# One placing stage for all four query blocks of a visit, value loads on SyncE's queue: a change to a fused attention and MLP kernel

## Chip, cores, metric

One core of one Trainium2 chip. The metric is the device time of the core in microseconds; each kernel was run several times beside the kernel before on the same chip.

## The reference

Attention with a threshold (8 batches, 8 heads, 576 positions, head size 64), then an MLP over 4608 tokens, all in fp32:

```python
scores = 0.125 * q @ k.T
scores = where(scores >= max(scores) - tau, scores, -1e9)
attn = softmax(scores)                    # then / (sum + 1e-9)
x = (attn @ v) laid out as (tokens, 512)
out = relu(x @ w_in) ** 2 @ w_out         # 512 -> 2048 -> 512
```

## The kernel before, in parts

Work goes in *visits*: two heads of one batch, in five steps (four blocks of 128 queries and a rest of 64). A step makes scores on TensorE, the softmax on VectorE, ScalarE and GpSimd, and fills the free time of TensorE with MLP matmuls from a list that is fixed when the program is built. The weights have to be turned (queries to columns) before the value products. From the twelfth visit on (25 visits) VectorE turns 32x32 tiles and DMAs **place** them in `wT`:

```python
def load_v(n):
    queue = nc.gpsimd if by_dma(n) else nc.sync
    ...                                     # 6 DMAs
def turn_blocks(vis, i):                    # pairs of blocks (0,1), (2,3), then the rest;
    ...                                     # two buffers in `turned`, used in turn
def place_blocks(vis, pair):
    for qb in range(4):
        for j in range(4):
            to = wT[j * 32:j * 32 + 32, :, :]
            if pair < NBLK // 2:            # 32 partitions x 9 runs of 64 floats
                nc.sync.dma_start(out=to[:, :, at:at + 64], in_=wb[rows, j::4, :, :]...)
            else:                           # the rest: 32 x (4 or 5) runs of 32 floats
                nc.sync.dma_start(out=to[:, c:c + n, at:at + 32], in_=wb[rows, first::4, 0, :])
...                                         # in step s, after the softmax of the step:
m, x = steps[s - 1]
turn_blocks(m, x)
if x >= 2:
    place_blocks(m, x - 2)                  # 16 DMAs at x = 2, 3 and 4
...                                         # end of the last step of a visit:
load_v(n + 1)
```

The value products of a visit (`mix`) stand four steps behind its last block; they read all of `wT`, so the next visit's DMAs can't start before they are done. `some_sums` makes 16 sums of MLP weights on VectorE once, just after the first of these visits.

Of the kernel before, what the change touches and what calls it, by code (L numbers as in the profile page):

```python
# [9 lines left out]
FP32 = mybir.dt.float32  # L10
# [9 lines left out]
def kernel(  # L20
# [10 lines left out]
    nc = tc.nc  # L31
    B, H, S, D = q.shape
    d_model, d_ff = moe_w_in.shape
    n_tokens = out.shape[0]
    P = 128
    HP = H // 2
    NPAIR = B * HP
    NBLK = S // P
    REST = S - NBLK * P
# [11 lines left out]
    const = ctx.enter_context(tc.tile_pool(name="const", bufs=1))  # L51
# [17 lines left out]
    WP = 512  # L69
# [3 lines left out]
    wT = const.tile([P, NC9, S], FP32, name="wT")  # L73
# [4 lines left out]
    at = RAW * 2 * WP  # L78
# [8 lines left out]
    RING = 6 * TCH  # L87
    xT = const.tile([P, NMC, RING], FP32, name="xT")
    KB = S // 32
    NB = 2 * KB * 2 * 32  # L90
    turned = const.tile([P, 2 * NB], FP32, name="turned")
    assert 3 * 3 * WP <= 2 * NB
    g = const.tile([P, NFT, TCH], FP32, name="g")
    gsum = [const.tile([P, HF, P], FP32, name=f"gsum{i}") for i in range(2)]
    p1s = const.tile([P, HD], FP32, name="p1s")
# [52 lines left out]
    def rows_of(n):  # L148
        return rows_in[n % 2 if n <= 2 * HP else 0]
# [16 lines left out]
    def load_v(n):  # L166
        b, h = divmod(visits[n][0], HP)
        h *= 2
        t = vs[n % 2]
        queue = nc.gpsimd if by_dma(n) else nc.sync  # L170
        for u in range(2):
            at = u * (NBLK + 1)
            queue.dma_start(out=t[:, at:at + NBLK, :],
                              in_=v[b, h + u, 0:NBLK * P, :].rearrange("(c p) d -> p c d", p=P))
            for half in range(2):
                queue.dma_start(out=t[half * D:(half + 1) * D, at + NBLK, :], in_=v[b, h + u, NBLK * P:S, :])

    def prep(n):

# [71 lines left out]
    def next_bank():  # L251

        among = (4, 5, 6, 7) if state["step"] > first_dma + 2 else (6, 7)
        used["bank"] = min([x for x in among if x > used["bank"]] or among)
        return bank[used["bank"]]
# [22 lines left out]
                nc.tensor.matmul(ps[rows, 0, 0:D], w[rows, 0, keys], ident[rows, rows], start=True, stop=True)  # L278
            nc.scalar.copy(wT[:, NBLK, NBLK * P:S], ps[:, 0, 0:D])

    blocks = {}
    N1 = 2 * P + REST

    def turn_blocks(vis, i):


        w = weights[vis, i][0]
        two = i < NBLK
        if not two or i % 2 == 0:
            at = len(blocks) % 2 * NB  # L290
            if two:
                wb = turned[:, at:at + NB].rearrange("p (k u q) -> p k u q", u=2, q=32)
            else:
                wb = turned[:, at:at + KB * 32].rearrange("p (k u q) -> p k u q", u=1, q=32)
            blocks[vis, i // 2] = wb
        wb = blocks[vis, i // 2]
        if two and i >= 2:

            parts = [(0, 0, KB - 2, 0), (0, KB - 2, KB, KB), (1, 0, 2, KB - 2), (1, 2, KB, KB + 2)]
        else:  # L300
            parts = [(u, 0, KB, u * KB) for u in range(2 if two else 1)]
        for u, k0, k1, at in parts:
            nc.vector.transpose(wb[:, at:at + k1 - k0, i % 2, :],  # L303
                                w[:, u, k0 * 32:k1 * 32].rearrange("p (k q) -> p k q", q=32))

    def place_blocks(vis, pair):


        wb = blocks[vis, pair]
        for qb in range(4):  # L310
            rows = slice(qb * 32, qb * 32 + 32)
            for j in range(4):
                to = wT[j * 32:j * 32 + 32, :, :]
                if pair < NBLK // 2:
                    at = pair * N1 + qb * 64
                    nc.sync.dma_start(out=to[:, :, at:at + 64], in_=wb[rows, j::4, :, :].rearrange("p c u q -> p c (u q)"))  # L316
                else:

                    first = j if qb < 2 else (j - KB) % 4
                    c = first // 4 if qb < 2 else (first + KB) // 4  # L320
                    n = len(range(first, KB, 4))
                    at = 2 * P + qb % 2 * 32
                    nc.sync.dma_start(out=to[:, c:c + n, at:at + 32], in_=wb[rows, first::4, 0, :])  # L323

    read_to = {"x": 0}

# [29 lines left out]
    def mix(n, cols):  # L356

        def term(ps, u, c, at, rows=slice(0, P), first=False, last=False):
            nc.tensor.matmul(ps[u * D:(u + 1) * D, :], vs[n % 2][rows, u * (NBLK + 1) + c, :],  # L359
                             wT[rows, NBLK if c == NBLK else u * (NBLK + 1) + c, at:at + ps.shape[1]],  # L360
                             start=first, stop=last)

        above, below = slice(0, D), slice(D, P)
        if not by_dma(n):
            ps = take("tx", (4, 5))[:, 0:cols.stop - cols.start]
            for c in range(NBLK):
                for u in range(2):
                    term(ps, u, c, cols.start, first=(c == 0))
            for u, rows in enumerate((above, below)):
                term(ps, u, NBLK, cols.start, rows, last=True)  # L370
            put(n, cols.start, ps, False)
            return
        one, two = (next_bank() for x in range(2))
        for c in range(NBLK):
            for ps, at in ((one[:, 0:N1], 0), (two[:, 0:S - N1], N1)):
                for u in range(2):
                    term(ps, u, c, at, first=(c == 0))

        for ps, at, places in ((one[:, 0:N1], 0, (above, below)), (two[:, 0:S - N1], N1, (below, above))):
            for u, rows in enumerate(places):  # L380
                term(ps, u, NBLK, at, rows, last=True)
        put(n, 0, one[:, 0:2 * P], True)
        put(n, NBLK * P, one[:, 2 * P:N1], False)
        put(n, 2 * P, two[:, 0:S - N1], True)

# [9 lines left out]
    def mlp_in(j, x):  # L395

        f, at = FORDER[x], j * TCH % RING
        if x % 2 == 0:
            used["h"] = take("mm", (6, 7)) if j < PLAIN else next_bank()
        h = used["h"].rearrange("p (f n) -> p f n", f=2)  # L400
        for c in range(NMC):
            nc.tensor.matmul(h[:, x % 2, :], w_in_sb[:, c, f * P:(f + 1) * P], xT[:, c, at:at + TCH],  # L402
                             start=(c == 0), stop=(c == NMC - 1))
        if x == NFT - 1:
            read_to["x"] = (j + 1) * TCH
        posts = []
        if j == PLAIN and state["step"] > first_dma + 1:
            posts.append(lambda: some_sums(2))
        if x % 2:
            def square():  # L410
                to = g[:, f - 1:f + 1, :]
                nc.scalar.activation(out=to, in_=h, func=AF.Relu)  # L412
                nc.gpsimd.tensor_tensor(out=to, in0=to, in1=to, op=ALU.mult)  # L413
                if j >= PLAIN and x % 8 == 7:
                    square_half(x // 8 * (HF // 2))
            posts.append(square)
        return posts
# [4 lines left out]
    def some_sums(count):  # L422

        for to, a, b, part in sums[:count]:
            f = slice(part * 2, part * 2 + 2)
            nc.vector.tensor_tensor(out=wo[:, to, f, :], in0=wo[:, a, f, :], in1=wo[:, b, f, :], op=ALU.subtract)  # L426
        del sums[:count]
# [27 lines left out]
    def product(j, x, half):  # L455
# [3 lines left out]
        to = used["p"][:, 0:HD]  # L459
        p = PRODUCTS[x]  # L460
        if sums:
            assert state["step"] > first_dma + 1
            some_sums(16 if x > 1 else 8)
        g0, g1 = g[:, 0:HF, :], g[:, HF:, :]
        left, slot = {"1": (g0[:, :, 0:P], Q00), "5": (gsum[0], FT1), "6": (gsum[1], FT2), "2": (g1[:, :, 0:P], Q10),
                      "7": (gsum[0], FT3), "4": (g1[:, :, P:], FT4), "3": (gsum[1], Q11)}[p]
# [42 lines left out]
    def by_dma(n):  # L509

        return n >= 3 * HP - 1
# [26 lines left out]
    PIECE_US = 1.76  # L538
    VALUES_US = 4.8
    waiting = deque()  # L540
    state = {"us": 0.0, "left": 0.0, "step": 0, "rounded": 0, "usable": 0, "then": [], "last": []}

    def early():
        return state["step"] < min(chunk_at)
# [77 lines left out]
    for s in range(END + 1):  # L622
# [5 lines left out]
        if on:  # L628
            n, i = steps[s]
            at = visits[n][1].index(i)  # L630
            last = at == len(visits[n][1]) - 1
            now = list(range(done, done + pieces[s]))
            done += pieces[s]
            more = n + 1 < len(visits)
            short = n < 2 * HP
            if short and at == 0 and 0 < n + 1 < 2 * HP:
                load_qk(n + 2)
            elif not short and at == 1 and more:
                load_qk(n + 1)
            if now:  # L640
                round_weights(now[0], 0)
            scores(s)
# [21 lines left out]
                add_chunk(j)  # L664
        if old:
            turn(*old, 2)
        if on:
            threshold(n, i)
            if last and more and not lay:
                prep(n + 1)  # L670
            if lay and now:
                round_weights(now[0], 1)
            if now:
                round_weights(now[0], 2)
                round_weights(now[0], 3)
            if not at_once:
                divide(n, i)
        if 0 < s <= NST and by_dma(steps[s - 1][0]):
            m, x = steps[s - 1]
            turn_blocks(m, x)  # L680
            if x >= 2:
                place_blocks(m, x - 2)
        fill(quarter)
        if on and at_once:
            divide(n, i)
# [48 lines left out]
```

## Time and profile before

| | before |
|---|---|
| time, median (range) | 1434.72 us (1434.34 to 1438.54), 3 runs |
| TensorE, VectorE, GpSimd busy | 96%, 61%, 53% |
| mean granted clock of TensorE | 0.991 |
| value products, wait for placing DMAs | 8.4 us, 5 times |

TensorE is the bound, so only its stops count. How the rows are read is told with the lines in the prediction. The list of DMA issues adds sizes and times to landing (columns: KB of one, median us from issue to landing):

```profile
wT<-turned SPq DMA_DIRECT2D x800, 72.0 KB, 2.2
...
vs<-in_v_dram POOLq DMA_DIRECT2D x50, 128.0 KB, 3.5
```

### The profile page before, as it was taken

Reading aid. Unit: us, or ns where it says so; the run is one execution under the profiler, and the core shown is the slowest. Engines: PE = TensorE matmul, PEld = TensorE weight load, DVE = VectorE, ACT = ScalarE, POOL = GpSimd, SP = SyncE. Lnnn points to the kernel's source line nnn. Section 1 sums busy time; section 2 is a strip of 40 time slices with the busy share of each in tenths; the row PEclk is TensorE's granted clock in tenths of the full one; section 3 lists DMA queues with packets and bytes.
Section 4 is the critical chain, followed back from the end, with each engine's and each line's share of the span. In section 5 each row is a group of like instructions: output and inputs, shape, how many; then the busy total and the mean of one; then the engine's idle time right before and its main releaser. Section 6 shows DMA issues by size and latency. Waiting matters only on the chain.

```text
span 1433.2 us, 22476 instructions
## 1 busy us (share of the span) xinstructions
PE 1374.8 (96%) x7460; PEld 1063.1 (74%) x7460; DVE 872.0 (61%) x1847; ACT 440.3 (31%) x1080; POOL 760.7 (53%) x1015
## 2 busy tenths in 40 slices
PE   5898999899999999999999999999999999999998
PEld 3676656677777777777777787777777877878887
DVE  5998886975766666666666666666666566401011
ACT  3765655223222323223232222222222232210100
POOL 2687887545555555655454646464546454422332
PEclk9998999999999999999999999999999999999999
DMA  7664541245555555554545555545454555310000
GB/s 149 131 141 108 130 115 41 48 79 106 90 108 94 108 98 113 99 105 87 94 87 106 92 102 98 111 86 101 81 102 89 104 95 111 67 29 12 4 15 15
DMA packets 507202, 127.14 MB, mean 89 GB/s; under 512 B 497488, under 2 KB 499088, under 8 KB 507088
## 3 DMA queue, kind: packets, MB, share of 16 engines
q1 hardware_dynamic: 496208, 107.78, 40.7%
q0 software_dynamic: 8496, 17.64, 4.0%
q8 instruction: 60, 0.98, 0.3%
q10 hardware_dynamic: 2384, 0.30, 0.1%
q14 instruction: 54, 0.44, 0.1%
HBM read 49.81 MB, written 9.44 MB: 41 GB/s over the span
## 4 chain that ended last, share of the span: by engine, by line
PE 80%; DVE 7%; SPq 5%; issue 2%; ACT 2%; DMA 1%; POOL 1%; ACTq 0%; POOLq 0%; DVEq 0%
PE bank L402 30%; PE bank L468 26%; PE s L202 12%; PE bank L359 10%; SPq L323 3%; SPq L316 2%; DVE w L230 1%; PE bank L266 1%; PE bank L436 1%; DVE st L207 1%; DVE wo L426 1%; DVE turned L138 1%; DVE turned L137 1%; ACT w L218 1%; DMA wT<-turned 1%
## 5 line engine op out<-in xcount | busy, mean ns | idle before, releaser
L402 PE MATMUL bank<-xT,w_in_sb 128*128 128x256 f32 x2304 | 521.8, 383 | 1.8 <-ACT osb L443 1.8
L402 PEld LDWEIGHTS bank<-xT,w_in_sb 128*128 128x128 f32 x2304 | 433.5, 191 | 82.8 <-issue 21.5
L207 DVE TENSOR_REDUCE st<-s 128x1 f32<-128x576 f32 x288 | 207.1, 753 | 221.1 <-PE s L202 219.7
L230 DVE SCALAR_TENSOR_TENSOR w<-s,st,w 128x576 f32<-128x576 f32 x269 | 210.1, 815 | 122.2 <-ACT w L218 122.0
L468 PE MATMUL bank<-wo,gsum 128*128 128x256 f32 x1088 | 248.7, 382 | 1.8 <-POOL gsum L392 1.7
L242 POOL TENSOR_SCALAR w<-w,st 128x576 f32<-128x576 f32 x269 | 225.8, 847 | 28.0 <-DVE st L233 21.1
L468 PEld LDWEIGHTS bank<-wo,gsum 128*128 128x128 f32 x1088 | 204.4, 190 | 40.0 <-issue 6.6
L413 POOL TENSOR_TENSOR g<-g 128x512 f32<-128x512 f32 x144 | 150.8, 1054 | 128.5 <-ACT g L412 128.2
L215 ACT ACTIVATE st<-st 128x2 f32<-128x2 f32 (+1 forms) x160 | 32.7, 204 | 603.5 <-DVE st L207 602.9
L202 PE MATMUL s<-kT,qT 64*128 64x288 f32 x1024 | 178.6, 445 | 36.0 <-DVE w L230 14.5
L468 PE MATMUL bank<-wo,g 128*128 128x256 f32 x816 | 187.9, 381 | 0.0
L359 PE MATMUL bank<-wT,vs 128*64 128x128 f32 (+7 forms) x1700 | 174.5, 358 | 11.8 <-DMA wT<-turned 8.4
L303 DVE STREAM_TRANSPOSE turned<-w 128x576 f32<-128x576 f32 (+2 forms) x325 | 167.7, 563 | 28.9 <-DMA wT<-turned 24.8
L218 ACT ACTIVATE w<-s,st 128x576 f32<-128x576 f32 x269 | 184.3, 731 | 0.6 <-issue 0.3
L468 PEld LDWEIGHTS bank<-wo,g 128*128 128x128 f32 x816 | 153.5, 190 | 28.1 <-issue 6.0
L240 POOL TENSOR_SCALAR st<-st 128x2 f32<-128x2 f32 (+1 forms) x160 | 36.8, 230 | 257.9 <-DVE w L230 247.0
L202 PEld LDWEIGHTS s<-kT,qT 64*128 64x128 f32 x1024 | 100.6, 193 | 96.0 <-issue 67.8
L359 PEld LDWEIGHTS bank<-wT,vs 128*64 128x64 f32 (+1 forms) x1700 | 101.6, 138 | 86.0 <-issue 39.0
L412 ACT ACTIVATE g<-bank 128x512 f32<-128x512 f32 x144 | 86.0, 599 | 180.1 <-PE bank L402 179.7
L482 DVE TENSOR_TENSOR gsum<-g 128x512 f32<-128x512 f32 x34 | 23.2, 715 | 109.3 <-PE bank L468 109.3
L185 POOL COPY qmid<-qT 64x64 f32<-64x64 f32 x64 | 18.7, 292 | 90.4 <-DVE qT L181 88.5
L143 POOL TENSOR_TENSOR turned<-turned 128x512 f32<-128x512 f32 x32 | 41.1, 1283 | 43.4 <-DVE turned L141 37.8
(68 smaller groups left out, 993.2 us busy)
## 6 DMA issues: line engine op xcount, KB each, us to landing
wT<-turned SPq DMA_DIRECT2D x800, 72.0 KB, 2.2
ql<-in_q_dram SPq DMA_DIRECT2D x126, 72.0 KB, 2.6
out_dram<-osb POOLq DMA_DIRECT2D x34, 256.0 KB, 2.8
wo<-in_moe_w_in_dram SPq DMA_DIRECT2D x16, 512.0 KB, 4.6
wo<-in_moe_w_out_dram SPq DMA_DIRECT2D x16, 512.0 KB, 3.8
vs<-in_v_dram POOLq DMA_DIRECT2D x50, 128.0 KB, 3.5
kl<-in_k_dram SPq DMA_DIRECT2D x63, 72.0 KB, 2.4
kl<-in_k_dram SPq DMA_DIRECT2D x63, 64.0 KB, 2.4
```

Source lines behind the costliest of these rows:

```text
L202: nc.tensor.matmul(sc[u][:, half, 0:HALF], lhsT, kT[rows, half * HALF:(half + 1) * HALF], start=True, stop=True)
L207: nc.vector.tensor_reduce(out=mx[:, u:u + 1], in_=sc[u][:, :, 0:HALF], axis=AX.XY, op=ALU.max)
L218: nc.scalar.activation(out=w[:, u, :].rearrange("p (h k) -> p h k", h=2), in_=sc[u][:, :, 0:HALF], func=AF.Exp, bias=bias[:, u:u + 1], sca ...
L230: nc.vector.scalar_tensor_tensor(out=wu, in0=sc[u][:, :, 0:HALF], scalar=thr[:, u:u + 1], in1=wu, op0=ALU.is_ge, op1=ALU.mult, accum_out=s ...
L242: nc.gpsimd.tensor_scalar(out=w[:, u, :], in0=w[:, u, :], scalar1=z[:, u:u + 1], scalar2=rcp[:, u:u + 1], op0=ALU.add, op1=ALU.mult)
L303: nc.vector.transpose(wb[:, at:at + k1 - k0, i % 2, :], w[:, u, k0 * 32:k1 * 32].rearrange("p (k q) -> p k q", q=32))
L323: nc.sync.dma_start(out=to[:, c:c + n, at:at + 32], in_=wb[rows, first::4, 0, :])
L359: nc.tensor.matmul(ps[u * D:(u + 1) * D, :], vs[n % 2][rows, u * (NBLK + 1) + c, :], wT[rows, NBLK if c == NBLK else u * (NBLK + 1) + c, a ...
L402: nc.tensor.matmul(h[:, x % 2, :], w_in_sb[:, c, f * P:(f + 1) * P], xT[:, c, at:at + TCH], start=(c == 0), stop=(c == NMC - 1))
L412: nc.scalar.activation(out=to, in_=h, func=AF.Relu)
L413: nc.gpsimd.tensor_tensor(out=to, in0=to, in1=to, op=ALU.mult)
L468: nc.tensor.matmul(to, left[:, f, :], wo[:, slot, f, :], start=(f == 0), stop=(f == HF - 1))
```

## The change

The intent: fewer and larger DMAs (runs of 512 B rather than 256), a less loaded SyncE queue, GpSimd freed of the value loads, and the weight sums spread over more steps. The four blocks share one buffer and are placed together when block 3 is turned; the rest is turned into the query tile, which is free by then, so the next q and k loads move one step later. The columns of `wT` now lie in another order, and a value product reads every other run of 64.

```diff
 def load_v(n):
-        queue = nc.gpsimd if by_dma(n) else nc.sync
...
-            queue.dma_start(out=t[:, at:at + NBLK, :],
+            nc.sync.dma_start(out=t[:, at:at + NBLK, :],
...
 def place_blocks(vis, i):
-                if pair < NBLK // 2:
-                    at = pair * N1 + qb * 64
-                    nc.sync.dma_start(out=to[:, :, at:at + 64], in_=wb[rows, j::4, :, :].rearrange(...))
+                if i < NBLK:
+                    nc.sync.dma_start(out=to[:, :, qb * P:(qb + 1) * P], in_=wb[rows, j::4, :])
...
 def mix(n, cols):
+            mov = wT[rows, NBLK if c == NBLK else u * (NBLK + 1) + c, :]
+                mov = mov.rearrange("p (g q) -> p g q", q=64)[:, at::2, :]
...
-        if j == PLAIN and state["step"] > first_dma + 1:
-            posts.append(lambda: some_sums(2))
+        if j == PLAIN and state["free"]:
+            posts.append(lambda: some_sums(1))
...
-            elif not short and at == 1 and more:
+            elif not short and at == (2 if by_dma(n) else 1) and more:
                 load_qk(n + 1)
...
             turn_blocks(m, x)
-            if x >= 2:
-                place_blocks(m, x - 2)
+            if x >= NBLK - 1:
+                place_blocks(m, x)
```

More of the change, by code (lines that the diff above doesn't have):

```diff
@@ L89 @@
     KB = S // 32
-    NB = 2 * KB * 2 * 32
-    turned = const.tile([P, 2 * NB], FP32, name="turned")
-    assert 3 * 3 * WP <= 2 * NB
+    turned = const.tile([P, 2 * KB * NBLK * 32], FP32, name="turned")
+    assert 3 * 3 * WP <= 2 * KB * NBLK * 32
     g = const.tile([P, NFT, TCH], FP32, name="g")
@@ L169, in load_v @@
         t = vs[n % 2]
-        queue = nc.gpsimd if by_dma(n) else nc.sync
         for u in range(2):
             at = u * (NBLK + 1)
-            queue.dma_start(out=t[:, at:at + NBLK, :],
+            nc.sync.dma_start(out=t[:, at:at + NBLK, :],
                               in_=v[b, h + u, 0:NBLK * P, :].rearrange("(c p) d -> p c d", p=P))
             for half in range(2):
-                queue.dma_start(out=t[half * D:(half + 1) * D, at + NBLK, :], in_=v[b, h + u, NBLK * P:S, :])
+                nc.sync.dma_start(out=t[half * D:(half + 1) * D, at + NBLK, :], in_=v[b, h + u, NBLK * P:S, :])
     def prep(n):
@@ L279, in turn, with place_blocks @@
             nc.scalar.copy(wT[:, NBLK, NBLK * P:S], ps[:, 0, 0:D])
-    blocks = {}
-    N1 = 2 * P + REST
     def turn_blocks(vis, i):
         w = weights[vis, i][0]
-        two = i < NBLK
-        if not two or i % 2 == 0:
-            at = len(blocks) % 2 * NB
-            if two:
-                wb = turned[:, at:at + NB].rearrange("p (k u q) -> p k u q", u=2, q=32)
-            else:
-                wb = turned[:, at:at + KB * 32].rearrange("p (k u q) -> p k u q", u=1, q=32)
-            blocks[vis, i // 2] = wb
-        wb = blocks[vis, i // 2]
-        if two and i >= 2:
-            parts = [(0, 0, KB - 2, 0), (0, KB - 2, KB, KB), (1, 0, 2, KB - 2), (1, 2, KB, KB + 2)]
-        else:
-            parts = [(u, 0, KB, u * KB) for u in range(2 if two else 1)]
-        for u, k0, k1, at in parts:
-            nc.vector.transpose(wb[:, at:at + k1 - k0, i % 2, :],
-                                w[:, u, k0 * 32:k1 * 32].rearrange("p (k q) -> p k q", q=32))
-    def place_blocks(vis, pair):
-        wb = blocks[vis, pair]
+        if i == NBLK:
+            parts = [(0, 0, KB, rows_of(vis)[0])]
+        else:
+            wb = turned.rearrange("p (k u q) -> p k u q", u=NBLK, q=32)[:, :, i, :]
+            if i >= 2:
+                parts = [(0, 0, KB - 2, 0), (0, KB - 2, KB, KB), (1, 0, 2, KB - 2), (1, 2, KB, KB + 2)]
+            else:
+                parts = [(u, 0, KB, u * KB) for u in range(2)]
+            parts = [(u, k0, k1, wb[:, at:at + k1 - k0, :]) for u, k0, k1, at in parts]
+        for u, k0, k1, to in parts:
+            nc.vector.transpose(to, w[:, u, k0 * 32:k1 * 32].rearrange("p (k q) -> p k q", q=32))
+    def place_blocks(vis, i):
+        wb = turned.rearrange("p (k u q) -> p k (u q)", u=NBLK, q=32) if i < NBLK else rows_of(vis)[0]
         for qb in range(4):
@@ L313, in place_blocks @@
                 to = wT[j * 32:j * 32 + 32, :, :]
-                if pair < NBLK // 2:
-                    at = pair * N1 + qb * 64
-                    nc.sync.dma_start(out=to[:, :, at:at + 64], in_=wb[rows, j::4, :, :].rearrange("p c u q -> p c (u q)"))
+                if i < NBLK:
+                    nc.sync.dma_start(out=to[:, :, qb * P:(qb + 1) * P], in_=wb[rows, j::4, :])
                 else:
@@ L321, in place_blocks @@
                     n = len(range(first, KB, 4))
-                    at = 2 * P + qb % 2 * 32
-                    nc.sync.dma_start(out=to[:, c:c + n, at:at + 32], in_=wb[rows, first::4, 0, :])
+                    at = NBLK * P + qb % 2 * 32
+                    nc.sync.dma_start(out=to[:, c:c + n, at:at + 32], in_=wb[rows, first::4, :])
     read_to = {"x": 0}
@@ L358, in term @@
         def term(ps, u, c, at, rows=slice(0, P), first=False, last=False):
-            nc.tensor.matmul(ps[u * D:(u + 1) * D, :], vs[n % 2][rows, u * (NBLK + 1) + c, :],
-                             wT[rows, NBLK if c == NBLK else u * (NBLK + 1) + c, at:at + ps.shape[1]],
-                             start=first, stop=last)
+            mov = wT[rows, NBLK if c == NBLK else u * (NBLK + 1) + c, :]
+            if by_dma(n):
+                mov = mov.rearrange("p (g q) -> p g q", q=64)[:, at::2, :]
+                to = ps[u * D:(u + 1) * D, :].rearrange("p (g q) -> p g q", q=64)
+            else:
+                mov = mov[:, at:at + ps.shape[1]]
+                to = ps[u * D:(u + 1) * D, :]
+            nc.tensor.matmul(to, vs[n % 2][rows, u * (NBLK + 1) + c, :], mov, start=first, stop=last)
         above, below = slice(0, D), slice(D, P)
@@ L373, in mix @@
         one, two = (next_bank() for x in range(2))
+        N1 = 2 * P + REST
         for c in range(NBLK):
-            for ps, at in ((one[:, 0:N1], 0), (two[:, 0:S - N1], N1)):
+            for ps, at in ((one[:, 0:N1], 0), (two[:, 0:S - N1], 1)):
                 for u in range(2):
                     term(ps, u, c, at, first=(c == 0))
-        for ps, at, places in ((one[:, 0:N1], 0, (above, below)), (two[:, 0:S - N1], N1, (below, above))):
+        for ps, at, places in ((one[:, 0:N1], 0, (above, below)), (two[:, 0:S - N1], 1, (below, above))):
             for u, rows in enumerate(places):
@@ L461, in product @@
         if sums:
-            assert state["step"] > first_dma + 1
-            some_sums(16 if x > 1 else 8)
+            need = {"5": 4, "6": 8, "4": 12, "7": 16}.get(p, 0)
+            some_sums(max(need - 16 + len(sums), 1))
+            assert state["free"]
         g0, g1 = g[:, 0:HF, :], g[:, HF:, :]
@@ L540 @@
     waiting = deque()
-    state = {"us": 0.0, "left": 0.0, "step": 0, "rounded": 0, "usable": 0, "then": [], "last": []}
+    state = {"us": 0.0, "left": 0.0, "step": 0, "free": False, "rounded": 0, "usable": 0, "then": [], "last": []}
     def early():
@@ L666 @@
             turn(*old, 2)
+        state["free"] = s > first_dma
         if on:
```

## The prediction

> **What bounds the kernel now.** I read the busy table by engine and slice first, then the windows of 35.83 us, then the waits, then the timelines of single engines around the stalls.
>
> ```profile
> PE 1374.8 (96%) x7460; PEld 1063.1 (74%) x7460; DVE 872.0 (61%) x1847; ACT 440.3 (31%) x1080; POOL 760.7 (53%) x1015
> ...
> PE   5898999899999999999999999999999999999998
> ...
> PEclk9998999999999999999999999999999999999999
> ```
>
> TensorE is the bound. Whatever stops it is added to the end, since the last 160 us are dense matmuls of the MLP alone. The idle 58 us lie in few places; the windows (us, PE busy, clock, DMA share, GB/s) name them:
>
> ```profile
> 0.00:35.83 35.83, 19.02 (x78) 1.00 0.76 149
> ...
> 250.81:286.64 35.83, 29.98 (x149) 0.90 0.26 48
> ...
> 322.47:358.30 35.83, 34.11 (x179) 1.00 0.56 106
> 358.30:394.13 35.83, 35.83 (x192) 1.00 0.50 90
> ...
> 1254.05:1289.88 35.83, 32.61 (x166) 1.00 0.13 29
> ```
>
> The first 240 us carry nothing of the change: the instruction orders of the two kernels agree there on every engine. Two places are left.
>
> First, the stop before 280 us, and the slow clock after it. The timelines of VectorE and TensorE:
>
> ```profile
> 268.04 7.80 DVE L426 TENSOR_TENSOR wo<-wo 128x512 f32<-128x512 f32 x6
> ...
> 267.51 7.07 PE L402 MATMUL bank<-xT,w_in_sb 128*128 128x256 f32 x32
> 280.43 2.29 PE L202 MATMUL s<-kT,qT 64*128 64x288 f32 x8 [5.85 <-DVE kT L181]
> 282.65 3.44 PE L402 MATMUL bank<-xT,w_in_sb 128*128 128x256 f32 x8
> ```
>
> The 16 weight sums (L426) sit in bursts of 4, 2, 6, 2, 2 in front of VectorE's softmax work. The scores of the next visit wait for its transposes. Then 8 matmuls take 3.44 us; elsewhere they take 1.99.
>
> Second, the value products of some visits wait for the placing DMAs. The waits (total, times, longest) and the timelines of TensorE, SyncE's queue and VectorE at one of them:
>
> ```profile
> PE bank L359 <- DMA wT<-turned: 8.4, 5, 3.2
> ...
> 344.99 0.75 PE L359 MATMUL bank<-wT,vs 128*64 128x320 f32 x2
> 347.46 4.75 PE L359 MATMUL bank<-wT,vs 128*64 128x320 f32 x38 [1.72 <-DMA wT<-turned]
> ...
> 312.74 21.87 SPq L316 DMA_DIRECT2D wT<-turned  x32
> 334.71 11.13 SPq L323 DMA_DIRECT2D wT<-turned  x16
> ...
> 320.09 1.52 DVE L303 STREAM_TRANSPOSE turned<-w 128x512 f32<-128x512 f32 x4
> ```
>
> The reader is to see that **the issue of the DMAs is the chain**, not their bytes. 48 DMAs leave SyncE one after the other in 33 us, at 0.68 us each. They start when the previous value products release wT at 312.7, and the last lands about 1.6 us after its issue. The next value products want wT at 345.
>
> **What the Trainium skill says.** "DMA: Bandwidth & Descriptors", section "Issuing engines are not separate DMA queues": issuing from several engines only saves the sequencer's issue time, usually small beside the DMA. The trace agrees on what is saved but not on small: a placing DMA holds SyncE for a median of 612 ns (plus about 40 ns between) and lands in 2.2 us. On the same page, "Why small descriptors are slow": a packet has a fixed overhead of about 3 cycles, so 256 B is 11 cycles; by that rule 512 B is 19 rather than 22, an estimate of 14% less DMA time for the blocks. Here 496,208 packets took 40.7% of 16 engines' 1433 us, 18.8 ns each, so an engine's 18 packets of one placing DMA (288 over 16) are some 0.34 us, under the issue interval: DMA engines are not what waits. "TensorE: Matmul & The Clock Gate", part 1: after an idle window of about 3.4 us the clock halves. The trace agrees: after 5.85 us of idling the matmuls are nearly twice as long. On moving operands read in runs of 64 columns I found no number; a 64-float run with a jump should stream at the same rate.
>
> **The change part by part.**
>
> 1. *Placing.* Per visit 16 + 16 + 16 DMAs become 16 (twice the bytes, runs of 512 B) + 16. The issue time doesn't follow size: L323 with 16 to 20 KB and L316 with 72 KB are both about 0.61 us. So SyncE saves 16 x 0.68 = 11 us per visit. But the 16 large ones can't start before block 3 is transposed. Before, half of the block work was issued by then.
>
> 2. *Value loads.* Six per visit go from GpSimd to SyncE. GpSimd loses 53.8 + 41.2 = 95 us of busy time, which is not the bound (53%) and hardly waited for by TensorE (1.7 us). SyncE gains six issues, 3.5 us as in the early part of the kernel (L173 and L176: 0.54 us each and gaps). In the order of SyncE's instructions of the changed kernel, they stand **between** the 16 block DMAs and the 16 of the rest.
>
> 3. *The chain this makes.* From the end of the transposes of block 3: 0.1 us to SyncE, 16 x 0.643 = 10.3, six value loads 3.5, 16 x 0.643 = 10.3, about 1.1 for the one or two slow issues that such a stretch has in this trace (32 measured 22.0 rather than 20.6), 1.55 from the last issue to TensorE's start: 26.8 us. TensorE's second value product (0.24 us after the first) needs all of it. In the shown visit the transposes end at 321.61 and the products start at 344.99, the second one 0.24 later: 23.6 us, so a delay of 3.2 us. From the same two timelines I took all 25 visits: four have 23.6 (3.2 us each = 12.8), seven have 25.35 (1.45 each = 10.2), three others 24.5, 25.6 and 25.9 (2.3 + 1.25 + 0.95 = 4.5), ten 26.4 or more (0 to 0.4), the last 23.1 but without value loads (about 0). Sum about 28 us. For the kernel before, comparing each value product stage with the 4.75 us of an undelayed one gives 2.43 + 2.04 + 2.01 + 1.52 + 0.52 + 0.14 + 1.55 + 3.93 = 14.1 us, of which the profile calls 8.4 idle. So this part **costs** about 14 us if the chain is 26.8. It is steep: 1 us less of chain makes it about zero.
>
> 4. *Sums.* The same 16, but 2 of them now fall into VectorE's gap of 8.15 us before 252, then 1, 2, 1, 3, 1, 3, 1, 2 after that. Adding VectorE's durations along this order (sums 0.64 to 1.3 us, as in the trace), the transposes that the scores wait for end near 274.6, about when TensorE is done: the stop of 5.85 us shrinks to 0 to 0.5, the slow clock after it (1.45 on the products and 1.05 on the scores) falls away, and a smaller stop of some 2.5 us comes one step later, at the second group of three. Gain: 5.85 + 2.5 - 2.7 = about 5.7 us.
>
> 5. *Rest.* The rest is transposed into the query tile, so the q and k loads move one step later. Before, they were issued at 345.9 behind the 48; now they come out behind the 38 at about the same time, well ahead of the 359 at which they are turned. TensorE's list is the same instruction for instruction. The one shared block buffer is free long before the next visit's block 0 (step after next), so VectorE's 24.8 us of waits for it should fall to a few, which TensorE doesn't feel.
>
> Sum: 1434.7 + 14 - 5.7 = 1443. I weigh the chain towards shorter (some loads issue in 0.4 us, and the slow issues may be fewer with 48 instead of 58 issues), and take **1440 us**.
>
> **Rivals.** (a) *The wait is gone.* With 38 issues after block 3 instead of 48 after the release of wT, the placing might be in time everywhere if the issue or the landing is faster than I take it (chain 24.5 or less leaves at most 1 us in four visits); then the gain is 14 + 5.7 and the time 1415 to 1420. For it: SyncE's queue is much emptier. Against it: only issues after block 3 count, and 38 x 0.65 alone is 24.7. (b) *The wait grows further*: 147 KB per DMA could bind on the engines (18 packets of 512 B at an estimated 36 ns, from 18.8 ns and the page's cycles, are 0.65 us, just the issue interval), or the value loads hold up; at 1 us more of chain some 15 to 20 us are added: 1455 to 1460. (c) *Strided reads or the single buffer slow TensorE or VectorE*: 1,000 value products at 10% more would be 9 us; nothing in the profile speaks for it. (d) *DMA is hidden anyway*: only the sums count, 1429.
>
> **Range and chances.** The chain is known to about 0.7 us, which is worth 10 us through 14 visits; the sums to 2 us. That gives 1424 to 1450. Two per cent are 28.7 us: below 1406 needs more than all that both places hold, above 1463 needs a chain over 28 us.
>
> **What would show it.** Right: the wait of the value products for the placing DMAs rises above 8.4 us, in more than 5 visits, with block 3's transposes followed at once by 16 issues, the value loads, 16 issues without a gap; L426 in small groups and the stop before 280 us below 1 us; packets down by about 115,000. Wrong: no wait at the value products (rival a), a placing DMA holding SyncE well over 0.65 us (b), matmuls of the value products longer than 438 and 380 ns (c).

## The result, and the profile after

1542.12 us (1537.64 to 1544.73, 4 runs) against 1436.23 us (4 runs): ratio 1.073, 95% interval 1.070 to 1.077. A ratio here is the mean time of one kernel's fast runs over that of the other's of the same rounds, so not quite the ratio of the medians. The change is 7% slower, and the prediction of 1440 (1424 to 1450) was wrong.

| | before | after |
|---|---|---|
| TensorE busy | 1374.8 us of 1433.2 | 1416.3 us of 1535.8 |
| mean granted clock | 0.991 | 0.971 |
| packets | 507,202 | 414,399 |
| 25 value product stages, beyond 4.72 us each | 14.1 us | 110.6 us |

The last row is the sum, over the visits with DMAs, of the time from the start of a visit's value products to TensorE's next work, less the 4.72 us of an undisturbed one. Its rise of 96.5 us is nearly all of the 102.6 us between the two profiled runs; another 4.5 us are waits for the same DMAs just ahead of the first product, in six of the visits. In the page, the row of slices and the chain that ended last (by line):

```profile
PE   5899999898989899899998998999999989999998
...
SPq L307 17%; SPq L314 14%; PE bank L357 11%; PE bank L399 11%; PE bank L466 11%; PE s L201 6%; DVE turned L296 3%; DMA vs<-in_v_dram 3%; DMA wT<-ql 3%; DVE w L229 2%; DVE st L206 2%; PE bank L433 1%; PE bank L265 1%; ACT w L217 1%; DVE tur
```

Slices of 80 to 90% now stand among the 9s of the middle, and SyncE's queue holds 31% of the chain, placing the blocks (L307) and the rest (L314), where it held 5%. The waits for the rest's DMAs (us in all, times, longest):

```profile
PE bank L357 <- DMA wT<-ql: 70.8, 30, 4.5
```

The timeline of TensorE, VectorE and SyncE's queue at the visit that the prediction took as its example (start, length, both us; in brackets the idle time ahead and what ended it):

```profile
346.46 0.72 PE L357 MATMUL bank<-wT,vs 128*64 128x320 f32 x2 [0.96 <-DMA wT<-ql]
351.63 7.09 PE L357 MATMUL bank<-wT,vs 128*64 128x320 f32 x38 [4.45 <-DMA wT<-ql]
358.65 1.99 PE L399 MATMUL bank<-xT,w_in_sb 128*128 128x256 f32 x8
...
319.90 1.52 DVE L296 STREAM_TRANSPOSE turned<-w 128x512 f32<-128x512 f32 x4
...
321.48 14.10 SPq L307 DMA_DIRECT2D wT<-turned  x16
335.62 0.80 SPq L172 DMA_DIRECT2D vs<-in_v_dram  x1
336.46 1.50 SPq L175 DMA_DIRECT2D vs<-in_v_dram  x2
338.01 0.59 SPq L172 DMA_DIRECT2D vs<-in_v_dram  x1
338.64 1.15 SPq L175 DMA_DIRECT2D vs<-in_v_dram  x2
339.89 10.34 SPq L314 DMA_DIRECT2D wT<-ql  x16
```

The reader is to see the predicted chain, link by link, only longer. Block 3 is turned at 321.42, the blocks go out at once, then the loads, then the rest without a gap, and TensorE goes on 1.4 us after the last issue ends. But the 16 block DMAs take 14.1 us here, and over the visits 12.5 to 14.2 (mean 13.0), where the prediction put 10.3 plus a slow issue. The loads take 4.2 where it put 3.5. From 321.42 to 351.63 are 30.2 us; it had said 26.8. And after the wait the 38 passes take 7.1 us rather than 4.5: the clock has dropped. The windows view shows it (stretch and its length; then busy us of TensorE, its weight load, VectorE, ScalarE and GpSimd with instructions; clock, DMA share, GB/s):

```profile
345.56:383.95 38.39, 33.04 (x162) 25.09 (x164) 18.04 (x42) 9.03 (x24) 18.01 (x23) 0.91 0.47 86
```

The mean clock of this visit's stretch is 0.91. The list of DMA issues shows the larger DMAs landing later:

```profile
wT<-turned SPq DMA_DIRECT2D x400, 144.0 KB, 3.5
```

The trace's records of single packets fit this: a packet of 512 B took 42.0 ns in the mean (115,200 of them), one of 256 B 22.1 ns on SyncE's queue in the kernel before (244,480, of which 230,400 are block copies). An engine has 18 of them per DMA, so 0.76 us, more than the 0.65 us in which SyncE issues. The issues of the blocks before and after, by source line (ns: shortest, median, longest):

```profile
L316 SPq DMA_DIRECT2D wT<-turned x800: 585/612/1837, 258.7 to 1253.8; - x160
...
L307 SPq DMA_DIRECT2D wT<-turned x400: 585/784/1850, 278.4 to 1357.2; - x134
```

By its place in the row of 16, an issue of L307 takes a median of 592 to 623 ns for the first four, as before, and 782 to 917 for the next six: the row gets slow only after its first DMAs. One rival can be excluded: each DMA first waits for the one eight before it to land, but for all 400 that one had landed at least 1.5 us earlier.

### The profile page after: what moved, and what is told of

Same layout as the page of the kernel before. It is cut to its first block, busy times and chain, and to the rows that moved or that the text cites. A ratio compares the mean times of both kernels' runs of the same rounds, so it can differ in the third digit from the quotient of the medians.

```text
span 1535.8 us, 21858 instructions
## 1 busy us (share of the span) xinstructions
PE 1416.3 (92%) x7460; PEld 1086.5 (71%) x7460; DVE 864.7 (56%) x1847; ACT 439.7 (29%) x1080; POOL 670.5 (44%) x865
## 2 busy tenths in 40 slices
DMA packets 414399, 127.09 MB, mean 83 GB/s; under 512 B 292689, under 2 KB 407889, under 8 KB 414289
## 4 chain that ended last, share of the span: by engine, by line
PE 42%; SPq 31%; DVE 12%; DMA 7%; issue 5%; ACT 3%; POOL 1%; DVEq 0%; ACTq 0%; POOLq 0%
SPq L307 17%; SPq L314 14%; PE bank L357 11%; PE bank L399 11%; PE bank L466 11%; PE s L201 6%; DVE turned L296 3%; DMA vs<-in_v_dram 3%; DMA wT<-ql 3%; DVE w L229 2%; DVE st L206 2%; PE bank L433 1%; PE bank L265 1%; ACT w L217 1%; DVE turned L138 1%
## 5 line engine op out<-in xcount | busy, mean ns | idle before, releaser
L399 PEld LDWEIGHTS bank<-xT,w_in_sb 128*128 128x128 f32 x2304 | 432.3, 190 | 81.9 <-issue 22.1
L357 PE MATMUL bank<-wT,vs 128*64 128x128 f32 (+7 forms) x1700 | 213.2, 395 | 73.8 <-DMA wT<-ql 70.8
L357 PEld LDWEIGHTS bank<-wT,vs 128*64 128x64 f32 (+1 forms) x1700 | 125.5, 150 | 163.8 <-issue 127.7
L296 DVE STREAM_TRANSPOSE turned<-w 128x576 f32<-128x576 f32 (+2 forms) x300 | 147.7, 543 | 43.7 <-DMA vs<-in_v_dram 42.8
```

Of the source, the lines that this page charges most:

```text
L296: nc.vector.transpose(to, w[:, u, k0 * 32:k1 * 32].rearrange("p (k q) -> p k q", q=32))
L357: nc.tensor.matmul(to, vs[n % 2][rows, u * (NBLK + 1) + c, :], mov, start=first, stop=last)
L399: nc.tensor.matmul(h[:, x % 2, :], w_in_sb[:, c, f * P:(f + 1) * P], xT[:, c, at:at + TCH], start=(c == 0), stop=(c == NMC - 1))
```

## Experiments

Theory A: the time is set by the row of issues on SyncE between block 3's transposes and the value products, and the loss is the excess of this chain over the 23.6 to 27 us that the products leave it, plus what a stop costs TensorE. Theory B: something else of the change (strided reads, the shared block buffer, late transposes) holds TensorE. The changed kernel's own trace already speaks against the strided reads: the first of its stages, which doesn't wait, takes 4.72 us from 307.74 on, as before.

"Stages" below is the sum over the 25 value product stages beyond 4.72 us each, from the profiled run.

**Value loads back on GpSimd.**

```diff
-            nc.sync.dma_start(out=t[...                # load_v of the changed kernel
+            (nc.gpsimd if by_dma(n) else nc.sync).dma_start(out=t[...
```

> The changed kernel with the value loads of the DMA visits back on GpSimd, nothing else. Theory A (the chain from block 3's transposes over SyncE to the value products sets the delay: 12.7 us of block DMAs, 4.2 of value loads, 10.3 of the rest, 1.5 to start): the chain falls by 4.2 to about 24.6 us, against 23.6 to 27 us that the products leave it. Delays at the value products fall from 110 us in sum to 5 to 15, the clock stays full, and the time is 1422 to 1438. Theory B (the strided reads, the shared block buffer or the slow clock hold TensorE whatever SyncE does): less than half of the loss goes, over 1490.

1447.57 us, ratio 1.008 (1.006 to 1.010); stages 26.1 us. 95 us of the loss are gone; the time is 10 us over Theory A's upper end. The blocks here took 12.6 to 14.7 us and landed 4.7 us after issue, not 3.5; that the loads, which now run beside them, are the reason was not tested (with the loads behind the rest, in the next run, they landed after 3.5).

**Value loads on SyncE, behind the rest.**

```diff
-            elif last and more and n >= 2 * HP:
-                load_v(n + 1)
+            elif last and more and n >= 2 * HP and not by_dma(n):
+                load_v(n + 1)
+            elif at == 0 and n > 2 * HP and by_dma(n - 1):
+                load_v(n)
```

> The changed kernel with the value loads still on SyncE, but one step later, behind the 16 DMAs of the rest. Theory A (only what stands ahead of the last placing DMA counts): the same as the run with the loads on GpSimd, 1422 to 1438. Rival (the six more issues load SyncE or the DMA engines as such, wherever they stand): stays over 1480.

1435.77 us, ratio 1.000 (0.998 to 1.002); stages 18.0 us. The same six issues on the same queue cost 106 us ahead of the rest and nothing behind it. It is their place in the row that counts, not the queue and not their load. These two runs also speak against the shared block buffer: VectorE waited 64.2 and 40.3 us for it, against 42.8 in the changed kernel, and yet the loss is gone.

**Value products one step later.**

```diff
-            mixed = {NBLK: (0, 4)}
+            mixed = {NBLK: (0, 5)}
```

> The changed kernel with the value products one step (about 8 us) later, nothing else. Theory A: the chain of 28.7 to 30.2 us now has 31.5 us or more, so hardly any delay stays; TensorE's work is the same: 1415 to 1428, faster than both kernels. Theory B (strided reads, shared buffer): over 1490.

1439.59 us, ratio 1.003 (1.000 to 1.006); stages 0.0. No product waits, as said, but the time is 12 us over the upper end. VectorE waits for the block buffer (46.8 us) and for query tiles (13.7 us), the scores come late (a stop of 2.23 us at 620 is the longest after 300 us), and the clock drops (0.91 between 360 and 400 us). So there seems to be a second limit behind the first, which the expectation missed; it was not isolated by a run of its own.

**Half the bytes.** The first form moved the columns of blocks 0 and 1 only.

```diff
-    nc.sync.dma_start(out=to[:, :, qb * P:(qb + 1) * P], in_=wb[rows, j::4, :])
+    nc.sync.dma_start(out=to[:, :, qb * P:qb * P + 64], in_=wb[rows, j::4, 0:64])
```

> The changed kernel with each block DMA moving only half of its columns (runs of 256 B; the result is wrong on purpose). If the bytes on the DMA engines (18 packets of 512 B at 42 ns each = 0.76 us) stretch the issue from 0.65 to 0.80 us, then the 16 issues take 10.3 to 11 us again, the chain is about 26.7 and the time is what the prediction's sum said, 1430 to 1450. If the number of issues is what counts and not the bytes: no change, about 1540.

1415.25 us, ratio 0.986 (0.984 to 0.988); stages 0. This run did not test what it was made for: DMAs that read only blocks 0 and 1 don't wait for block 3, so they started 9 us earlier (307.70 in the example visit, where block 3 is turned at 316.56). What it does show is the time without any wait at the products: about 1415 us.

**Half the bytes, but of blocks 2 and 3.**

```diff
+    nc.sync.dma_start(out=to[:, :, qb * P + 64:(qb + 1) * P], in_=wb[rows, j::4, 64:])
```

> The changed kernel with each block DMA moving only the columns of blocks 2 and 3 (runs of 256 B, half the bytes; wrong result on purpose). Unlike the earlier half-size run, the DMAs still have to wait for block 3's transposes, since they read its columns. Theory A with bytes: 16 issues in 10.6 us, loads 3.7, rest 10.4, 1.5 to start: a chain of 26.2 us, delays of 15 to 35 us in sum, 1435 to 1455. If the bytes do not matter: 1530 to 1545. If only the late start mattered, it would not differ from the changed kernel either.

1458.72 us, ratio 1.014 (1.011 to 1.017); stages 44.0 us. The time is 4 us over the upper end. SyncE's queue in the example visit:

```profile
318.98 10.56 SPq L307 DMA_DIRECT2D wT<-turned  x16
329.59 0.60 SPq L172 DMA_DIRECT2D vs<-in_v_dram  x1
330.23 1.17 SPq L175 DMA_DIRECT2D vs<-in_v_dram  x2
331.45 0.59 SPq L172 DMA_DIRECT2D vs<-in_v_dram  x1
332.08 1.15 SPq L175 DMA_DIRECT2D vs<-in_v_dram  x2
333.33 11.69 SPq L314 DMA_DIRECT2D wT<-ql  x16
```

Sixteen issues of the same form with half the bytes take 10.56 us rather than 14.10, and the loads behind them 3.6 rather than 4.2. The number of DMAs, the number of packets and the wait for block 3 are unchanged; only the packets are half as long. The median issue is 612 ns again, and 592 to 617 at all 16 places of the row. So the bytes stretch the issue, and they are worth 83 us (1542 to 1459).

**The kernel before with the value loads on SyncE.**

```diff
-        queue = nc.gpsimd if by_dma(n) else nc.sync
+        queue = nc.sync
```

> The kernel before with the value loads on SyncE, nothing else. Theory A (SyncE's row of issues is the chain): there the chain runs from the end of one visit's value products to the next: 34.8 us with 48 placing DMAs, and the loads stand ahead of the rest, so 38.4 to 39; the products leave it 33 to 36 us. Every visit then waits, 3 to 6 us and some slow clock: 1490 to 1545. Rival (the loads only hurt together with the 512-byte runs, by the DMA engines): under 1450.

1520.88 us, ratio 1.060 (1.056 to 1.063); stages 105.9 us, 25 of 25 waiting. One line of the change alone costs 85 us, without any 512-byte run. In the example visit 32 block issues take 22.1 us, the loads 3.65, the rest 10.34; from 311.4 to TensorE's start at 349.04 are 37.6 us.

**The kernel before with the sums spread.**

> The kernel before with only the weight sums spread as in the changed kernel. By the prediction 5.7 us faster (1430). By the trace of the changed kernel the stop before the scores falls from 5.85 to 0.9 us, but 4 us come back at once: a wait of 2.3 us for GpSimd's gsum and a slow clock behind it. So 1 to 3 us faster, 1433 to 1436, within the noise.

1433.01 us, ratio 0.998 (0.996 to 1.000): 2 to 3 us, barely clear of noise. (The edit is the `some_sums` part of the change.) The lines in the changed kernel that told this beforehand:

```profile
276.98 1.24 PE L201 MATMUL s<-kT,qT 64*128 64x288 f32 x8 [0.88 <-DVE kT L180]
...
291.23 7.13 PE L466 MATMUL bank<-wo,gsum 128*128 128x256 f32 x24 [2.28 <-POOL gsum L389]
```

The stop of 5.85 us is 0.88 us, but TensorE then comes to GpSimd's sums earlier, waits 2.28 us for them, and runs 24 matmuls in 7.13 us (5.45 in the kernel before). In this run's own trace the stop is 0.87 us and the wait for GpSimd only 0.69; there the gain is taken back one step after the stop, where TensorE waits 1.49 us for VectorE and then runs 8 score matmuls in 2.55 us rather than 1.24 and 8 of the next in 3.03 rather than 1.99.

**Both terms of the chain away.** The half DMAs of blocks 2 and 3, and the value loads behind the q and k loads (`load_v(n)` at `at == 2`).

> Both terms of the chain away at once: block DMAs with half the bytes that still wait for block 3 (wrong result on purpose), and the value loads behind the q and k loads. Theory A: 10.7 + 10.6 + 1.5 = 22.8 us, under 23.6: no delay at the products, and the time of the run without any waits, 1412 to 1420. If something else than the chain holds the products (reads, shared buffer, late transposes): over 1430.

1418.41 us, ratio 0.989 (0.986 to 0.991); stages 1.0 us. The example visit: 16 issues in 10.59 us from 318.24, the rest from 328.93 to 339.19, and the products start at 341.56 and run through. Shared buffer, strided reads and late start are all still there. VectorE's wait for the buffer did shrink with the bytes (3.7 us), but the two runs with the loads moved had it in full without the loss. Together they settle Theory A against B.

**Looking for a version that beats both.** First, the changed kernel with the products a step later and the loads behind the q and k loads (both edits shown).

> A version to beat both: value products one step later, and the value loads behind the q and k loads at the end of SyncE's row. In the run with only the products later no product waited, but VectorE waited 46.8 us for the block buffer and 13.7 us for q tiles and the scores came late. With 4.2 us less ahead of the rest and of the q and k loads the q waits should go and the scores come in time: 1414 to 1426. If the wait for the block buffer is what holds the scores, it stays (16 us after block 3's transposes in both): 1432 to 1442.

1429.58 us, ratio 0.996 (0.994 to 0.998); stages 0. Faster than the kernel before by 0.4%, which the interval shows, and between the two expected ranges. The wait for query tiles is 1.8 us. What is left of the second limit may be VectorE's wait for the block buffer, 3.7 us in the run of 1418 us above; it was not tested alone:

```profile
DVE turned L296 <- DMA wT<-ql: 35.0, 23, 3.8
```

Then 4 of the 16 DMAs of the rest on ScalarE's queue, once in the changed kernel (with the loads last), once in the kernel before:

```diff
+    (nc.scalar if j == 3 else nc.sync).dma_start(out=to[:, c:c + n, at:at + 32], ...)
```

> The changed kernel with the value loads behind the q and k loads and 4 of the 16 DMAs of the rest issued by ScalarE's queue. Theory A: SyncE's chain is 13 (blocks) + 8 (12 of the rest) + 1.5 = 22.5 us, under the 23.6 that the shortest visit leaves, so no product waits unless ScalarE's four come later (2.6 us of its row, behind its own work). 1414 to 1424, faster than both. Rival: ScalarE, kept 2.6 us in each visit, delays the exponents and evictions: 1430 or more, with waits of TensorE for ScalarE.

> The kernel before with 4 of the 16 DMAs of the rest on ScalarE's queue, nothing else. Theory A: its chain of 34.8 us from one visit's products to the next loses 2.6, and the eight delays (14 us in sum) mostly go: 1421 to 1428. Rival (ScalarE is held too long): 1436 or more.

1450.07 us (1.010, 1.009 to 1.012) and 1457.90 us (1.016, 1.014 to 1.019): both expectations of Theory A failed, and the times are those of the rival. (No run has the first kernel with only its loads moved like this; with the loads one step later it took 1435.77.) The stages shrank as said (4.6 and 10.5 us), so the chain did get shorter. But the waits of the first of them show ScalarE standing before work of its own:

```profile
ACT g L409 <- DMA wT<-ql: 52.3, 10, 6.8
ACT st L214 <- DMA wT<-ql: 19.6, 3, 6.6
```

In the instruction list every DMA of the two queues waits first for an earlier one of a round of eight, whichever of them that was on; this fits ScalarE being kept not 2.6 us but up to 6.8, with evictions and exponents late. TensorE's own waits don't name ScalarE, as the rival had said, but those for VectorE's exponents are longer (24.9 us in the first, 18.1 in the changed kernel).

## Why the prediction was wrong

- **The bound and the chain: right.** TensorE is the bound, and SyncE's row of issues from block 3's transposes on, with the value loads in the middle, is what the products wait for. The link order and the point where it starts are as predicted, within 0.2 us (321.4 against 321.6 in the example).
- **The term that failed: 10.3 us for 16 block issues.** It rested on "The issue time doesn't follow size", drawn from 16 to 72 KB, and on "DMA engines are not what waits". At 144 KB both are false: 13.0 us in the mean. Half the bytes bring it back to 10.9 (10.6 in the example) and the time to 1459. Rival b had named the case and put the packet at an estimated 36 ns, 0.65 us per DMA, "just the issue interval". It was 42 ns and 0.76 us. The working fails at both of its inputs. The 18.8 ns is a mean over all packets of the queue, from 4 B up; those of 256 B took 22.1 in the same trace, and twice that is 44. And "the page's cycles" are 11 for 256 B and, by the same rule, 19 for 512 B: from "DMA: Bandwidth & Descriptors", "Why small descriptors are slow (HBM only)", which says that copies from SBUF to SBUF don't suffer this penalty. Here they took 42.0 / 22.1 = 1.90 times as long, nearly double, in line with that; the cycles would give 1.73, and with 18.8 ns not 36 but 32.5. An estimate that lands exactly on the limit should have widened the range, not closed the question.
- **A small term: the loads.** 4.2 us rather than 3.5, because they too stand behind busy engines (3.65 behind the half DMAs). Together the chain is 28.6 to 31.0 us (mean 29.4), not 26.8: 24 of 25 visits wait, not 14.
- **What a wait costs: too low.** The delays were taken as landing less readiness. With the chain about as predicted (the run with half the bytes of blocks 2 and 3), they should have come to about 28 us; the stages lost 44, of which only 23 are idle time. A stop costs TensorE its idle time, about 0.7 us more until it runs full (6.97 - 4.72 - 1.53 in the stage at 705.6 us), and in many cases a slow clock for the rest of the stage. In the changed kernel 16 of 24 stopped stages lost 2.0 us or more beyond their idle time, all with a mean clock of 0.69 to 0.85; the other eight, at full clock, lost 0.71 to 0.72. The prediction had used the slow clock for the sums and not for its own waits.
- **The sums: right at the stop, wrong in the gain.** The stop fell to 0.88 us; of 5.7 us some 2.5 came. The smaller stop one step later was foreseen (2.5 us; it took 1.49); the slow clock behind it (some 2.3 us in the run with the sums alone) and, in the changed kernel, the wait for GpSimd's gsum (2.28 us) were not.
- **Right:** strided reads cost nothing (4.72 us), the packets of the blocks fell by 115,200 as predicted (in all by 93,000 only, for the value loads came to SyncE's queue as more and smaller packets), GpSimd's relief gave nothing that a run shows.
- **Wrong, and without effect here:** VectorE's waits for the block buffer were to fall from 24.8 us to a few. They rose to 42.8 (3.7 in the run with half the bytes and the loads last); TensorE's waits for VectorE ahead of the scores did not grow (36.6 us before, 34.5 after).
- **The range.** The text called the dependence steep, 1 us of chain for 14 us, and took the chain as known to 0.7 us. The runs give more than 30 us per us: from 27.0 us of chain in the mean (half the bytes) to 29.4 the time rose by 83.

What stays open: 12 of the 122 us between the changed kernel and the one without waits are outside the value product stages; 4.5 of them are the waits ahead of the first product, and the rest (slow clock around the stages, by the look of the timeline) was not taken apart. That the issue gets longer with the bytes is shown, and that it does so from the fifth DMA of a row on; by what mechanism is not.

## What to carry to other kernels

When DMAs leave one queue in a row and something waits for the last, count every issue ahead of it, and put loads that are needed later behind it: the same six loads cost 106 us in front and nothing behind. Merging two DMAs into one saved less than half of the issue time here (16 in 13.0 us against 32 in 22), since an engine's share of one (0.76 us) was longer than the issue interval (0.65 us), and it delayed the first until the last input was ready. If a wait sits at the edge of what is hidden, check both the slope and what a stop costs afterwards before calling the range narrow.

## What the Trainium skill lacked or had wrong

- "DMA: Bandwidth & Descriptors", "Issuing engines are not separate DMA queues": issue time is called usually small beside the DMA. Here it is 0.61 us of 2.2, and 38 to 48 of them in a row are a chain of 25 to 33 us. No page says that an issue gets longer with the bytes of a row of DMAs: median 612 ns with 72 KB, 784 ns with 144 KB.
- "TensorE: Matmul & The Clock Gate", part 1, gives an idle window of about 3.4 us. Here a stop of 2.28 us (393.4 us in the changed kernel) was followed by 38 passes in 6.4 us rather than 4.5, while one of 3.18 us (879.6 us) was not. In the changed kernel's stages all seven stops of 0.95 to 1.58 us left the clock full, and of the 17 from 2.02 to 4.46 us all but that one took it. Stops well under the window can cost the clock too.
- No page gives what a stop in a row of fp32 matmuls costs besides idle time and clock: 0.71 to 0.72 us in each of the eight stopped stages that kept the full clock.
